# Attention and gated-FFN block on one core: W_k loaded transposed in five blocks, its fold in one stretch, W_q's blocks moved into the loop

## The chip, the core and the metric

The kernel runs on one core of a Trainium2 chip. The metric is device time in microseconds: the median over executions of the whole program. Four executions of the kernel before gave 279.43, 279.59, 280.50 and 281.14 us, with a median of 280.05 us.

A core has five engines that run side by side, each in its own program order: PE (TensorE, matrix products; PEld is its weight load), DVE (VectorE), ACT (ScalarE), POOL (GpSimd) and SP (SyncE). In this kernel all transfers are issued from SP's queue; the profile calls its issuing time SPq. An engine waits for another, or for a transfer, on a semaphore, and everything queued behind a waiting instruction on the same engine waits too.

## The reference

One batch of 2048 rows of width D = 640, in bf16:

```
x = A_x                                    # (1, 2048, 640)
def A(x):                                  # attention, 32 heads of width 20
    q, k, v = split(x @ wqkv)              # each (32 heads, 2048, 20)
    pq, pk = q @ w_phi[h], k @ w_phi[h]    # per head, 20 x 20
    phi_q = concat(softmax(pq), softmax(-pq))
    phi_k = concat(softmax(pk), softmax(-pk))
    kv, z = phi_k^T @ v, sum_s phi_k
    o = (phi_q @ kv) / (phi_q . z + 1e-6)
    return o @ wo
def B(x):
    return (gelu(x @ w_gate) * (x @ w_up)) @ w_down    # F = 1536
h   = x + A(layernorm(x))
out = h + B(layernorm(h))
```

## The kernel before, in words

The 2048 rows are 16 tiles of 128 rows. `x_sb[b]` holds four tiles; `LN1T[b]` holds their layernormed rows transposed, so that the 640 features lie in five chunks of 128 partitions. The first stage, which the change touches, takes up the first 26 us or so; behind it come the rest of a loop over the 16 tiles (k, v and the sum phi_k^T v), the q side, and the attention output woven into the FFN. Those later stages are long runs of matrix products on PE and are not edited, apart from the loop's passes 0 to 4.

**The fold.** The per-head product with `w_phi` is linear, so it is folded into the weights: `Wk2 = W_k · blockdiag(w_phi)`, and `Wq2` likewise. `fold` (L210) takes the weight transposed (`WkT`, `WqT`) and the block diagonals `BD`, which DVE builds from `wphi` and a mask (L391). A fold of one block d of 128 rows is six matmuls into a PSUM tile `wa` and one copy out of it: on ACT for the blocks named in `KA` (`QA` for W_q), otherwise on DVE (L232 to L235). W_k's fold must be over before the first k product; W_q's blocks are folded in passes 4 to 8 (`FQ`).

**Transfers.** SP issues, in this order: tiles 0, 1, 3 of x, W_v in three pieces with tile 2 of x between them, `wphi` (L178), tiles 4 and 5 (L179), the whole of W_k transposed on its way in (L180), tiles 6 and 7 (L181), tiles 8 to 11 (L185), the whole of W_q transposed (L186), tiles 12 to 15 (L187). After that SP issues the transposes of layernormed tiles 6 to 15 (`LN1T`, L148), each of which waits for its tile.

**Tiles 0 to 5.** Their layernormed rows are transposed on PE (`ln_tp`: five transposes into a PSUM tile `tp`, then a copy to `LN1T` on DVE or ACT). `ln_st` is the statistics on DVE with the reciprocal root on ACT (`log=True`) or POOL; `ln_ap` applies them. Tile 3's statistics come from two ACT passes (`st3_act`) and a short POOL chain. v of tiles 0 to 3 is computed ahead of the loop, from PSUM tile `pv` to `vS` on ACT (`v_ev`).

**Order.** All engines run in the order in which the program is written (`manual_schedule`); no planner moves anything. PE's order from tile 2 on is: transposes of tile 2, rest of v(1), part of v(2), transposes of tile 3, rest of v(2), half of v(3), fold of W_k's blocks 0 and 1, other half of v(3), fold of blocks 2 to 4, transposes of tile 4. Pass t of the loop then does k(t), in passes 4 to 8 a fold of W_q, on odd passes from 5 on two tiles of kv, and v(t+4). Pass 0 has tile 5's transposes between k(0) and v(4). Pass t also prepares the layernormed tile t+6: pass 0 on DVE, later ones on ACT. All PSUM tiles of this stage share four buffers in rotation (`gtile`).

Of the kernel before, what the change touches and what calls it, by code (L numbers as in the profile page):

```python
# [10 lines left out]
ALU = mybir.AluOpType  # L11
# [6 lines left out]
def kernel(  # L18
# [12 lines left out]
    nc = tc.nc  # L31
    P = 128
# [13 lines left out]
    NH = [(P * c + P - 1) // Dh - H0[c] + 1 for c in range(NC)]  # L46
    NWARM = 10
    VP = (0, 2, 4, 6, 9, 11)
    KA, QA = (0,3), (0,1,2,3,4)
    FQ = (4, 5, 6, 7, 8)  # L50

    QG = ((0, 1), (2, 3), (4, 5), (6,), (7, 8), (9, 10), (11, 12), (13, 14), (15,), (16,), (17,), (18,), (19,))
# [124 lines left out]
    nc.sync.dma_start(Wv[:, 4:5, :], w_v[:, 4:5, 2 * D:3 * D])  # L177
    nc.sync.dma_start(wphi, phi_v.rearrange("(c p) f -> p c f", p=P))  # L178
    nc.sync.dma_start(x_sb[1][:, 0:2, :], x_v[:, 4:6, :])  # L179
    nc.sync.dma_start_transpose(WkT, A_wqkv[:, D:2 * D])  # L180
    nc.sync.dma_start(x_sb[1][:, 2:4, :], x_v[:, 6:8, :])  # L181
    wo_v = A_wo.rearrange("(c p) n -> p c n", p=P)
    wg_v = B_w_gate.rearrange("(c p) n -> p c n", p=P)
    wu_v = B_w_up.rearrange("(c p) n -> p c n", p=P)
    nc.sync.dma_start(x_sb[2], x_v[:, 8:12, :])  # L185
    nc.sync.dma_start_transpose(WqT, A_wqkv[:, 0:D])  # L186
    nc.sync.dma_start(x_sb[3], x_v[:, 12:16, :])  # L187


    zero = fp.tile([P, 512], BF16, name="zero")  # L190
# [19 lines left out]
    def fold(WT, W2, halves, ds=range(NC)):  # L210


        runs = []
        for c in range(NC):
            lo, hi = H0[c] * Dh, (H0[c] + NH[c]) * Dh
            for u in range(2):
                a, b = max(lo, u * HD), min(hi, (u + 1) * HD)
                if a < b:
                    runs.append((u, c, a, b))
        runs.sort()  # L220
        for d in ds:
            wa = gtile("wa")
            for i, (u, c, a, b) in enumerate(runs):
                nc.tensor.matmul(wa[:, u, a - u * HD:b - u * HD], lhsT=WT[:, c, d * P:(d + 1) * P],  # L224
                                 rhs=BD[:, c].rearrange("p a b -> p (a b)")[:, a - H0[c] * Dh:b - H0[c] * Dh],
                                 start=(i == 0 or runs[i - 1][0] != u),
                                 stop=(i + 1 == len(runs) or runs[i + 1][0] != u), skip_group_check=True)
            dst, src = W2[:, d, :].rearrange("p (u f) -> p u f", u=2), wa[:, :, 0:HD]
            if halves:
                dst = W2[:, d, :].rearrange("p (c u f) -> p u c f", c=NC, u=2)  # L230
                src = src.rearrange("p u (c f) -> p u c f", c=NC)
            if d in (QA if halves else KA):  # L232
                nc.scalar.copy(dst, src)
            else:
                nc.vector.tensor_copy(dst, src)  # L235
# [3 lines left out]
    def ln_st(*tiles, act=True, between=None, log=False):  # L239
        for t, v in zip(tiles, ln_stats(p1, [x_sb[t // 4][:, t % 4, :] for t in tiles], "1", act, between, log)):  # L240
            lnp[t] = v

    def ln_ap(t, on_act=False, on_pe=False):
        ln = (ln_act if on_act else ln_dve)(p1, "1", *lnp[t])
        if on_pe:
            lnp[t] = ln
        else:
            transpose_to(LN1T[t // 4][:, :, t % 4 * P:(t % 4 + 1) * P], ln, False)

    def ln_tp(t, on_dve=False):  # L250
        transpose_to(LN1T[t // 4][:, :, t % 4 * P:(t % 4 + 1) * P], lnp[t], True, on_dve)
# [13 lines left out]
    def v_mm(t, us=(0, 1)):  # L265
        if 0 in us:
            pv[t] = gtile("pv")
        proj(pv[t], t, Wv, us)

    def v_part(t, *cs):  # L270

        if 0 in cs:
            pv[t] = gtile("pv")
        for c in cs:
            for u in range(2):
                nc.tensor.matmul(pv[t][:, u, 0:HD], lhsT=lnT(t, c), rhs=Wv[:, c, u * HD:(u + 1) * HD],
                                 start=(c == 0), stop=(c == NC - 1))

    def v_ev(t):
        nc.scalar.copy(vS[t % 8][:, :, 0:Dh].rearrange("p (u h) f -> p u h f", u=2),  # L280
                       pv[t][:, :, 0:HD].rearrange("p u (h f) -> p u h f", f=Dh))
# [13 lines left out]
    def k_norm(t):  # L295


        sk = small(p1, [P, 2 * H], "sk")
        nc.vector.reduce_sum(sk, Ek[t].rearrange("p s (h f) -> p (s h) f", f=Dh), axis=AX.X)  # L299
        if t - 1 in todo:  # L300
            todo.pop(t - 1)()
        rs = small(p1, [P, 2 * H], "rs")
        nc.vector.reciprocal(rs, sk)  # L303
        Vt[t] = vt = ev.tile([P, 2, H, VC], BF16, name="vt", bufs=8)

        def mult(s, eng):
            eng.tensor_tensor(vt[:, s], vS[t % 8], rs[:, s * H:(s + 1) * H, None].to_broadcast([P, H, VC]), ALU.mult)  # L307

        mult(1, nc.gpsimd)
        if t in VP:  # L310
            mult(0, nc.gpsimd)
        elif t == NT - 1:
            mult(0, nc.vector)
        else:
            todo[t] = lambda: mult(0, nc.vector)
# [38 lines left out]
    def st3_act(i):  # L354

        xt = x_sb[0][:, 3, :]
        nc.scalar.activation(sq3, xt, (ACTF.Square, ACTF.Identity)[i], accum_out=sm3[:, i:i + 1])
        if i == 1:
            nc.gpsimd.tensor_scalar(v3[:, 0:1], sm3[:, 1:2], sm3[:, 1:2], -1.0 / (D * D), op0=ALU.mult, op1=ALU.mult)
            nc.gpsimd.tensor_scalar_add(v3[:, 0:1], v3[:, 0:1], EPS)  # L360
            nc.gpsimd.tensor_scalar(v3[:, 1:2], sm3[:, 0:1], 1.0 / D, v3[:, 0:1], op0=ALU.mult, op1=ALU.add)
            nc.gpsimd.tensor_tensor(v3[:, 2:3], v3[:, 1:2], nhalf[:, 0:1], op=ALU.pow)
            nc.gpsimd.tensor_scalar(v3[:, 3:4], sm3[:, 1:2], 1.0 / D, None, op0=ALU.mult)
            lnp[3] = xt, v3[:, 3:4], v3[:, 2:3], None
# [2 lines left out]
    sm3 = fp.tile([P, 2], F32, name="sm3")  # L367
    v3 = fp.tile([P, 4], F32, name="v3")

    def st1_between():  # L370
        st3_act(0)
        ln_ap(0, on_pe=True)

    ln_st(0, act=False, log=True)
    ln_st(1, act=False, between=st1_between, log=True)
    st3_act(1)
    ln_tp(0, True)
    warm(WA)
    ln_ap(1, on_pe=True)
    v_part(0, 0, 1)  # L380
    ln_tp(1)
    ln_st(2, act=False, log=True)
    v_part(0, 2, 3, 4)
    v_ev(0)
    v_part(1, 0, 1, 2)
    ln_ap(2, on_pe=True)
    ln_ap(3, on_pe=True)
    ln_tp(2, True)
    ln_st(4, act=False)

    nc.vector.tensor_tensor(BD, wphi[:, :, None, :].to_broadcast([P, NC, 8, Dh]),  # L391
                            hmask[:, :, :, None].to_broadcast([P, NC, 8, Dh]), ALU.mult)
    v_part(1, 3, 4)
    v_ev(1)
    v_part(2, 0, 1)
    ln_tp(3)
    v_part(2, 2, 3, 4)
    v_ev(2)
    ln_ap(4, on_pe=True)
    ln_st(5, act=False)  # L400
    v_mm(3, (0,))
    fold(WkT, Wk2, False, (0, 1))
    v_mm(3, (1,))
    v_ev(3)
    fold(WkT, Wk2, False, (2, 3, 4))
    ln_ap(5, on_pe=True)
    ln_tp(4)
    ln_st(6)
    ln_st(7)
    fp_cm.__exit__(None, None, None)  # L410
    ev_cm = tc.tile_pool(name="ev", bufs=1, side="right", reuse_waits="tile")
# [2 lines left out]
    for t in range(NT):  # L414
        if t == T3:
            ps_cm.close()
            psG = ps_cm.enter_context(tc.tile_pool(name="psG", bufs=3, space=PSUM, reuse_waits="tile"))
            psK = ps_cm.enter_context(tc.tile_pool(name="psK", bufs=1, space=PSUM, reuse_waits="tile"))
            kvp = psK.tile([P, 2, 512], F32, name="kvp")
        k_tile(t)  # L420
        if t == 0:
            ln_tp(5)
            ln_ap(6)
        if t in FQ:
            fold(WqT, Wq2, True, [i for i, f in enumerate(FQ) if f == t])
        for j in range(len(QT)):
            if t == QT[j]:
                q_mm(j)
                q_exp(j)
        if t % 2 == 1 and t >= 5:  # L430
            kv_tile(t - 5)
            kv_tile(t - 4)
        if t + 4 < NT:
            v_mm(t + 4)
        if t > 0 and t + 6 < NT:
            ln_ap(t + 6, on_act=True)
        if t + 4 < NT:
            v_ev(t + 4)
        if t % 2 == 0 and t + 8 < NT:
            ln_st(t + 8, t + 9)  # L440
        k_norm(t)
        if t == 9:
            nc.gpsimd.memset(KV, 0.0)
            nc.gpsimd.memset(kmask, 1.0)
            for r in HALF:
                nc.gpsimd.affine_select(out=kmask[r], in_=kmask[r], pattern=[[4, NC], [-Dh, 4]],
                                        compare_op=ALU.is_ge, fill=0.0, base=0, channel_multiplier=1)
                nc.gpsimd.affine_select(out=kmask[r], in_=kmask[r], pattern=[[-4, NC], [Dh, 4]],
                                        compare_op=ALU.is_ge, fill=0.0, base=Dh - 1, channel_multiplier=-1)
            nc.gpsimd.tensor_copy(KV[:, :, 0, :, KC - 1], kmask)  # L450
            nc.gpsimd.tensor_copy(KV[:, :, 1, :, 0], kmask)
        if t == 10:
            nc.sync.dma_start(Wg, wg_v)
            nc.sync.dma_start(Wo, wo_v)
            nc.sync.dma_start(Wu, wu_v)
# [282 lines left out]
```

The softmax here doesn't subtract the row's maximum and nothing guards it: scores larger than these inputs give would overflow.

## Time and profile before

The profiled execution took 281.14 us, the longest of the four; its span, first to last instruction, is 279.40 us, so 1.74 us lie around it.

| what | value |
|---|---|
| median of 4 runs | 280.05 us |
| profiled execution, and its span | 281.14 us, 279.40 us |
| PE busy | 272.1 us, 97% of the span |
| DVE, ACT, POOL busy | 165.1, 143.0, 95.7 us |
| granted TensorE clock | 1.00 |
| DMA queue of SP | 20.68 MB, 30.5% of 16 engines |

How to read it: a row of the timeline gives the start and the length in us, the engine, the source line, what is written from what, and in brackets how long the engine had been idle and who ended that. A row's length of several matmuls includes the drain of the last one, so successive rows can overlap. "To landing" is the time from the start of a transfer's issue on SP until its last piece has been signalled. The chain of work that ended last is followed back from the last instruction: a piece on it that gets shorter shortens the span unless another chain takes over.

### The profile page before, as it was taken

Reading aid. Unit: us, or ns where it says so; the run is one execution under the profiler, and the core shown is the slowest. Engines: PE = TensorE matmul, PEld = TensorE weight load, DVE = VectorE, ACT = ScalarE, POOL = GpSimd, SP = SyncE. Lnnn points to the kernel's source line nnn. Section 1 sums busy time; section 2 is a strip of 40 time slices with the busy share of each in tenths; the row PEclk is TensorE's granted clock in tenths of the full one; section 3 lists DMA queues with packets and bytes.
Section 4 is the critical chain, followed back from the end, with each engine's and each line's share of the span. In section 5 each row is a group of like instructions: output and inputs, shape, how many; then the busy total and the mean of one; then the engine's idle time right before and its main releaser. Section 6 shows DMA issues by size and latency. Waiting matters only on the chain.

```text
span 279.4 us, 5780 instructions
## 1 busy us (share of the span) xinstructions
PE 272.1 (97%) x2322; PEld 172.4 (62%) x2337; DVE 165.1 (59%) x289; ACT 143.0 (51%) x239; POOL 95.7 (34%) x211
## 2 busy tenths in 40 slices
PE   7898999999999999999999999999999999999995
PEld 3575777774645788788864555675455567444574
DVE  5699997789397686676324848322657632333222
ACT  5577999768598847355624454412446350222200
POOL 3438996694401315555401244310135230000000
PEclk9999999999999999999999999999999999999999
DMA  7997122694350021314120113131031513000011
GB/s 210 179 228 179 38 48 49 148 395 189 95 191 0 2 48 26 69 38 99 34 70 2 32 21 69 38 82 47 2 47 23 74 25 94 26 0 0 0 49 47
DMA packets 40635, 21.05 MB, mean 75 GB/s; under 512 B 33440, under 2 KB 38816, under 8 KB 40608
## 3 DMA queue, kind: packets, MB, share of 16 engines
q1 hardware_dynamic: 40608, 20.68, 30.5%
q8 instruction: 18, 0.29, 0.4%
q14 instruction: 9, 0.07, 0.1%
HBM read 10.18 MB, written 2.62 MB: 46 GB/s over the span
## 4 chain that ended last, share of the span: by engine, by line
PE 89%; DMA 4%; DVE 3%; SPq 1%; POOL 1%; issue 1%; POOLq 0%
PE gu L588 37%; PE pd L609 19%; PE pq L347 8%; PE po L543 8%; PE pk L260 6%; PE pv L260 5%; PE ab L483 3%; PE kvp L325 2%; DMA x_sb<-in_A_x_dram 2%; DMA LN1T<-ln 2%; DVE stats L108 1%; DVE Wk L235 1%; PE wa L224 1%; DVE ln L137 0%; POOL rstd L121 0%
## 5 line engine op out<-in xcount | busy, mean ns | idle before, releaser
L594 DVE TENSOR_TENSOR GT<-gu,g 128x512 bf16<-128x512 f32 (+1 forms) x60 | 34.4, 580 | 54.3 <-ACT g L591 54.1
L591 ACT ACTIVATE g<-gu 128x512 bf16<-128x512 f32 (+1 forms) x60 | 30.7, 512 | 69.4 <-PE gu L588 68.2
L588 PE MATMUL gu<-LN2T,Wg 128*128 128x512 bf16 (+1 forms) x289 | 61.3, 335 | 0.7
L588 PE MATMUL gu<-LN2T,Wu 128*128 128x512 bf16 (+1 forms) x300 | 61.7, 336 | 0.0
L609 PE MATMUL pd<-Wd,GT 128*128 128x320 bf16 (+2 forms) x396 | 53.8, 295 | 0.0
L609 PEld LDWEIGHTS <-GT 128*128 128x128 bf16 x396 | 38.0, 98 | 15.3 <-DVE GT L594 0.9
L588 PEld LDWEIGHTS <-Wu 128*128 128x128 bf16 x300 | 29.4, 98 | 22.6
L588 PEld LDWEIGHTS <-Wg 128*128 128x128 bf16 x300 | 28.4, 98 | 20.7
L260 PEld LDWEIGHTS <-LN1T 128*128 128x128 bf16 x290 | 27.6, 98 | 12.4 <-DMA LN1T<-ln 1.5
L307 POOL TENSOR_TENSOR vt<-vS,rs 128x672 bf16<-128x672 bf16 x22 | 29.7, 1372 | 9.2 <-DVE rs L303 8.5
L614 DVE TENSOR_TENSOR y<-pd,x_sb 128x640 bf16<-128x640 f32 (+3 forms) x18 | 13.5, 749 | 30.2 <-PE pd L609 30.2
L491 ACT COPY AB<-ab 128x704 f32<-128x704 f32 x28 | 19.6, 748 | 19.8 <-PE ab L483 19.6
L299 DVE TENSOR_REDUCE sk<-E 128x64 f32<-128x1280 bf16 x16 | 23.1, 1446 | 4.2 <-ACT E L292 4.2
L524 DVE TENSOR_TENSOR tt<-AB,w 128x1280 bf16<-128x1280 f32 x16 | 23.8, 1485 | 1.1 <-POOL w L517 0.9
L543 PE MATMUL po<-Wo,oT 128*128 128x320 bf16 x160 | 24.3, 299 | 0.0
L260 PE MATMUL pk<-Wk,LN1T 128*128 128x320 bf16 x160 | 24.2, 299 | 0.0
L292 ACT ACTIVATE E<-pk 128x640 bf16<-128x640 f32 x32 | 20.9, 707 | 6.5 <-PE pk L260 6.3
L347 PE MATMUL pq<-LN1T,Wq 128*128 128x512 bf16 x96 | 22.7, 379 | 0.2
L260 PE MATMUL pv<-Wv,LN1T 128*128 128x320 bf16 x130 | 20.0, 299 | 1.2 <-DMA LN1T<-ln 1.2
L352 ACT ACTIVATE Eq<-pq 128x1024 bf16<-128x1024 f32 (+1 forms) x26 | 19.9, 830 | 2.4 <-PE pq L347 2.4
L543 PEld LDWEIGHTS <-oT 128*128 128x128 bf16 x160 | 15.6, 98 | 7.0 <-ACT oT L146 0.3
L132 ACT ACTIVATE ln<-x_sb,v,rstd 128x640 bf16<-128x640 bf16 x14 | 12.9, 919 | 11.3 <-POOL v L571 11.1
(89 smaller groups left out, 264.0 us busy)
## 6 DMA issues: line engine op xcount, KB each, us to landing
out_dram<-y SPq DMA_DIRECT2D x15, 160.0 KB, 1.8
Wg<-in_B_w_gate_dram SPq DMA_DIRECT2D x1, 1920.0 KB, 7.6
Wu<-in_B_w_up_dram SPq DMA_DIRECT2D x1, 1920.0 KB, 14.9
Wd<-in_B_w_down_dram SPq DMA_DIRECT2D x1, 1920.0 KB, 7.9
x_sb<-in_A_x_dram SPq DMA_DIRECT2D x2, 640.0 KB, 5.5
Wo<-in_A_wo_dram SPq DMA_DIRECT2D x1, 800.0 KB, 9.3
x_sb<-in_A_x_dram SPq DMA_DIRECT2D x4, 160.0 KB, 2.8
Wv<-in_A_wqkv_dram SPq DMA_DIRECT2D x2, 320.0 KB, 4.1
```

Source lines behind the costliest of these rows:

```text
L260: nc.tensor.matmul(ps[:, u, 0:HD], lhsT=lnT(t, c), rhs=W[:, c, u * HD:(u + 1) * HD], start=(c == 0), stop=(c == NC - 1))
L292: nc.scalar.activation(Ek[t][:, s, :].rearrange("p (u f) -> p u f", u=2), pk[:, :, 0:HD], ACTF.Exp, scale=(1.0 if s == 0 else -1.0))
L299: nc.vector.reduce_sum(sk, Ek[t].rearrange("p s (h f) -> p (s h) f", f=Dh), axis=AX.X)
L307: eng.tensor_tensor(vt[:, s], vS[t % 8], rs[:, s * H:(s + 1) * H, None].to_broadcast([P, H, VC]), ALU.mult)
L347: nc.tensor.matmul(pqs[j][:, i, :], lhsT=Wq2[:, kc, c * P:(c + 1) * P], rhs=LN1T[b][:, kc, :], start=(kc == 0), stop=(kc == NC - 1))
L352: nc.scalar.activation(Eq[j][:, :, s, :], pqs[j][:, 0:len(QG[j])], ACTF.Exp, scale=(1.0, -1.0)[s])
L524: nc.vector.tensor_tensor(tt.rearrange("p s (h f) -> p s h f", f=Dh), num, w[:, :, :, None].to_broadcast([P, 2, H, Dh]), ALU.mult)
L543: nc.tensor.matmul(po[:, u, 0:HD], lhsT=st[t][:, c, :], rhs=Wo[:, c, u * HD:(u + 1) * HD], start=(c == 0), stop=(c == NC - 1))
L588: nc.tensor.matmul(gu[:, i, 0:n], lhsT=W[:, c, f * P:(f + 1) * P], rhs=LN2T[b][:, c, a0:a1], start=(c == 0), stop=(c == NC - 1))
L591: nc.scalar.activation(g[:, 0:n], gu[:, 0, 0:n], ACTF.Gelu_apprx_tanh)
L594: nc.vector.tensor_tensor(st[b, "g", f][:, a0:a1], gu[:, 1, 0:n], g[:, 0:n], ALU.mult)
L609: nc.tensor.matmul(pd[:, u, n0:n1], lhsT=st[b, "g", f][:, tl * P:(tl + 1) * P], rhs=Wd[:, f, u * HD + n0:u * HD + n1], start=(f == 0), sto ...
```

## The change

W_k is loaded transposed by five transfers of 128 rows each in place of one. The loads of tiles 6 to 15 are written behind v(2), but on SP they follow the five W_k blocks directly. W_q is loaded by five such transfers too, one at the end of each of the passes 0 to 4, behind the transpose of layernormed tile t+6 on SP's queue.

The block diagonals are built in two pieces, chunks 0 to 2 and chunks 3 and 4, with tile 2's layernorm between them; both are now ahead of tile 4's statistics on DVE. Tile 3's two ACT passes come later: the first behind tile 1's, the second behind tile 2's reciprocal root. Tile 3's layernorm comes behind tile 4's statistics.

On PE, v(2) is one stretch, then W_k's blocks 0, 1 and 2 are folded, then tile 3's transposes, then blocks 3 and 4, then v(3) in one stretch, then tile 4's transposes; tile 5's transposes come behind v(4) in pass 0. ACT copies out blocks 1 and 3, in place of 0 and 3. On DVE the statistics of tiles 5 and 6 come ahead of the layernorm of tile 5.

```diff
-    KA, QA = (0,3), (0,1,2,3,4)
+    KA, QA = (1,3), (0,1,2,3,4)
...
-    nc.sync.dma_start_transpose(WkT, A_wqkv[:, D:2 * D])
-    nc.sync.dma_start(x_sb[1][:, 2:4, :], x_v[:, 6:8, :])
+
+    def load_T(WT, i, *ds):
+
+        for d in ds:
+            nc.sync.dma_start_transpose(WT[:, :, d * P:(d + 1) * P], A_wqkv[d * P:(d + 1) * P, i * D:(i + 1) * D])
+
+    load_T(WkT, 1, *range(NC))
...
-    nc.sync.dma_start(x_sb[2], x_v[:, 8:12, :])
-    nc.sync.dma_start_transpose(WqT, A_wqkv[:, 0:D])
-    nc.sync.dma_start(x_sb[3], x_v[:, 12:16, :])
...
-    def st1_between():
-        st3_act(0)
-        ln_ap(0, on_pe=True)
+    def bd(c0, c1):
+
+        n = c1 - c0
+        nc.vector.tensor_tensor(BD[:, c0:c1], wphi[:, c0:c1, None, :].to_broadcast([P, n, 8, Dh]),
+                                hmask[:, c0:c1, :, None].to_broadcast([P, n, 8, Dh]), ALU.mult)
 
     ln_st(0, act=False, log=True)
-    ln_st(1, act=False, between=st1_between, log=True)
-    st3_act(1)
+    ln_st(1, act=False, between=lambda: ln_ap(0, on_pe=True), log=True)
+    st3_act(0)
     ln_tp(0, True)
     warm(WA)
     ln_ap(1, on_pe=True)
     v_part(0, 0, 1)
     ln_tp(1)
     ln_st(2, act=False, log=True)
+    st3_act(1)
     v_part(0, 2, 3, 4)
     v_ev(0)
+    bd(0, 3)
+    ln_ap(2, on_pe=True)
+    bd(3, NC)
     v_part(1, 0, 1, 2)
-    ln_ap(2, on_pe=True)
-    ln_ap(3, on_pe=True)
     ln_tp(2, True)
     ln_st(4, act=False)
-
-    nc.vector.tensor_tensor(BD, wphi[:, :, None, :].to_broadcast([P, NC, 8, Dh]),
-                            hmask[:, :, :, None].to_broadcast([P, NC, 8, Dh]), ALU.mult)
+    ln_ap(3, on_pe=True)
     v_part(1, 3, 4)
     v_ev(1)
-    v_part(2, 0, 1)
-    ln_tp(3)
-    v_part(2, 2, 3, 4)
+    v_part(2, *range(NC))
     v_ev(2)
+    nc.sync.dma_start(x_sb[1][:, 2:4, :], x_v[:, 6:8, :])
+    nc.sync.dma_start(x_sb[2], x_v[:, 8:12, :])
+    nc.sync.dma_start(x_sb[3], x_v[:, 12:16, :])
+    fold(WkT, Wk2, False, (0, 1, 2))
+    ln_tp(3, False)
+    fold(WkT, Wk2, False, (3, 4))
+    v_mm(3)
+    v_ev(3)
     ln_ap(4, on_pe=True)
+    ln_tp(4)
     ln_st(5, act=False)
-    v_mm(3, (0,))
-    fold(WkT, Wk2, False, (0, 1))
-    v_mm(3, (1,))
-    v_ev(3)
-    fold(WkT, Wk2, False, (2, 3, 4))
+    ln_st(6)
     ln_ap(5, on_pe=True)
-    ln_tp(4)
-    ln_st(6)
     ln_st(7)
...
         if t == 0:
-            ln_tp(5)
             ln_ap(6)
...
             v_mm(t + 4)
+            if t == 0:
+                ln_tp(5)
...
         k_norm(t)
+        if t < NC:
+            load_T(WqT, 0, t)
```

## The prediction, made before the changed kernel was run

> **What bounds the kernel now.** I read the page first, for who carries the span: PE, busy 97%. So time can only come from the few places where PE stands still. The second view is the chain that ended last, in order of time: from 25.29 us on it is PE alone, without a wait worth naming, and ahead of that it runs through transfers and DVE.
>
> ```profile
> PE 272.1 (97%) x2322; PEld 172.4 (62%) x2337; DVE 165.1 (59%) x289; ACT 143.0 (51%) x239; POOL 95.7 (34%) x211
> ```
>
> ```profile
> 4.63 6.37 DMA x_sb<-in_A_x_dram
> 11.00 0.02 issue
> 11.02 0.90 DVE stats L108 x2
> ...
> 20.31 4.93 DMA LN1T<-ln
> 25.25 0.05 issue
> 25.29 1.53 PE pv L260 x10
> 26.82 1.36 PE pk L260 x10
> ```
>
> So the span is 25.29 us plus a PE stream that the change leaves as long as it is; what counts is when v(6), the product at 25.29, can start. The timeline of PE shows the two stalls before it, 0.80 us for W_k transposed and 1.16 us for tile 6's transpose:
>
> ```profile
> 13.97 0.80 PE L224 MATMUL wa<-BD,WkT 128*128 128x140 bf16 x12 [0.80 <-DMA WkT<-in_A_wqkv_dram]
> ...
> 22.61 1.52 PE L260 MATMUL pk<-Wk,LN1T 128*128 128x320 bf16 x10
> 25.29 1.53 PE L260 MATMUL pv<-Wv,LN1T 128*128 128x320 bf16 x10 [1.16 <-DMA LN1T<-ln]
> ```
>
> SP's queue tells why. The two whole transposes hold SP for 6.74 and 5.66 us, x's last tiles are issued only at 18.78, and tile 6's transpose at 20.31 lands 4.93 us later where the next two took 2.6:
>
> ```profile
> 5.20 6.74 SPq L180 DMA_TRANSPOSE WkT<-in_A_wqkv_dram  x1
> 11.99 0.57 SPq L181 DMA_DIRECT2D x_sb<-in_A_x_dram  x1
> 12.60 0.43 SPq L185 DMA_DIRECT2D x_sb<-in_A_x_dram  x1
> 13.07 5.66 SPq L186 DMA_TRANSPOSE WqT<-in_A_wqkv_dram  x1
> 18.78 0.58 SPq L187 DMA_DIRECT2D x_sb<-in_A_x_dram  x1
> ```
>
> Last, the rows of tile `wphi`, for the new position of the block diagonals. It lands at 4.15 + 5.6 = 9.75 us:
>
> ```profile
> L178 SPq DMA_DIRECT2D wphi<-in_A_w_phi_dram x1: 433/433/433, 4.2 to 4.2; - x1
> ...
> DMA to landing us min/median/max: 5.6/5.6/5.6
> ```
>
> **The change, step by step.** All times are in the profiled execution (281.14 us, span 279.40, 1.74 around it). The pace of PE is from the chain: a v or k product 1.36, a folded block 0.32, five transposes 0.28.
>
> *Block diagonals ahead of tile 2's layernorm.* DVE is done with tile 2's statistics at 8.15. It then waits for `wphi` until 9.77; before, it could go on at 8.99, when ACT's root was ready. Behind the wait are tile 2's layernorm, the second piece, the copy of tile 2's transposes and tile 4's statistics; PE waits for the first. The whole takes 0.94 us for 800 elements. For 480 I bound it by 0.56 (proportional) and 0.94 (no cheaper than the whole), and take 0.60, nearer the proportional end, since the width falls by two fifths. So: piece one 9.77 to 10.37, layernorm (0.45) to 10.79, and PE's transposes of tile 2 start at 10.85 instead of 9.50. By the rows of before the copy starts 0.55 after the layernorm's end and takes 0.49: 11.34 to 11.83. The second piece (0.41) fits while PE transposes. v(2) starts at 11.88 against 10.53: 1.35 us lost here, with PE idle for some 1.25 us from 9.6.
>
> *Tile 4's statistics and tile 3.* Statistics 11.77 to 12.90 (0.89 and 0.21); their data are there at 11.0, so that wait of before is gone. Tile 3's ACT passes end near 9.8, POOL's five steps (7.34 to 9.16 before, 1.82) near 11.7; its layernorm runs at 12.86 to 13.30, where it hides beside v(2). v(0)'s copy moves from 8.87 to 9.8 behind the ACT pass; its buffer is next wanted by v(2), so this costs nothing.
>
> *PE from v(2) on.* v(2) to 13.25; blocks 0 to 2 to 14.21; tile 3's transposes to 14.5; blocks 3 and 4 to 15.14. ACT copies v(2) (0.69), block 1, then tile 3's transposes until 15.34, so v(3) starts at 15.39, a stall of 0.25. It ends at 16.75; transposes of tile 4 (layernorm on DVE at 15.95 to 16.40, behind its third copy of a fold) to 17.03; k(0) from 17.03. Ahead of v(6) PE then has what it had before, k(0), v(4), tile 5's transposes, k(1), v(5) and k(2): 17.03 + 5 × 1.36 + 0.28 = 24.11.
>
> *W_k in five blocks.* SP: each block bounded by 1.20 (a tile's transpose of the same shape) and 6.74/5 = 1.35, so the last is issued by 11.4 to 11.9, against 11.94. The landing of block 4 is bounded below by 10.2 + 2.6 = 12.8 (a lone tile transpose) and, if the bytes come as those of the whole, by 13.9 (5.20 + 8.7). I take 13.9: both share the queue with x. It is wanted at 14.82, block 2 at 13.89, by which the whole would be nearly down. Hidden, with 0.9 us of cover.
> The Trainium skill, "DMA: Bandwidth & Descriptors", section "Anatomy of one DMA", gives each transfer about 2.0 us of fixed cost and so speaks against cutting one transfer into five; charged one after the other, the four more would bring block 4 to an estimated 13.9 + 8.0 = 21.9 us, 7.1 behind its need, and the result to some 6 us slower. This trace has four loads of x and W_v issued within 1.4 us of each other, at 0.79 to 2.18, landing 2.3 to 3.9 us after issue, so such costs overlap here.
>
> *Loads of x.* They follow W_k at 11.4 to 11.9, 12.5 and 13.0. Tiles 12 to 15 are thus issued 5.8 us sooner, and with 5.2 to 5.8 us to landing, as before, are down by 19, ahead of tile 6's transpose.
>
> *Tile 6.* DVE: block 0 copied 13.62 to 14.43, block 2 to 15.15, block 4 to 16.0 (0.81 each, some 0.74 apart), tile 4's layernorm to 16.4, statistics of 5 and 6 to 18.5, layernorm 5, statistics of 7 to 19.85, layernorm 6 to 20.30: the time of before, 20.28, by coincidence. Its transpose is issued at 20.35 with nothing ahead of it; 2.6 us bring it to 22.95, under 24.11 by 1.16. The wait of 1.16 is gone.
>
> *W_q in the loop.* Five issues of 1.20 on SP, each behind the transpose of a tile and ahead of the next one's. ACT ends tile 7's layernorm at 23.57 as before, while SP is free from about 22.8; blocks 1 to 4 likewise fall into the 2 to 4 us between SP's transposes. Block 0 lands near 24.2 and is folded near 29.5, block 4 near 37 and is folded near 43.8. Cost nothing; the cover is SP's gap. Without it a tile transpose comes 1.2 later. Tile 7 lands at 26.2, wanted at 26.83; tile 8 at 28.9, wanted at 29.87. Before, that slack was 1.8 and 2.1 us.
>
> **Sum.** Taken away: stalls of 1.16 and 0.80, and idle ends of early products that the rows show as busy; added: 1.25 at tile 2 and 0.25 at tile 3. All together v(6) goes from 25.29 to 24.11, −1.18 us. ACT, DVE and POOL keep up: DVE works ahead of PE's needs by some 4 us at the kv products, and ACT's passes are as long as before. So 281.14 becomes 279.96. The profiled execution lies 1.09 above the median; the same 1.18 off 280.05 gives 278.9 us, 0.4% less. A difference under 0.5%, 1.4 us, is about what a measurement of this kernel can't tell from none.
>
> **Rivals.**
> *More is won: `wphi` comes sooner.* The stretches from 9.0 to 10.5 us show the transfers nearly idle, 7, 10 and 26 GB/s, with a piece of x and of `wphi` still out, so an execution without that hole is possible. `wphi` can't be sooner than the W_v piece ahead of it, 3.64 + 4.3 = 7.94. At 8.2 v(2) starts at 10.5 as before and the folds are next held by W_k's last block, 13.9: 0.9 us more, 278.0.
> *Given back in the loop.* Slack at tiles 7 and 8 falls to 0.6 and 1.0, and of ten tile transposes before two took 4.2 us to land; one such at tile 7 costs 1.6 − 0.6 = 1.0. Then −0.2: 279.9. Against it: both slow ones came after 30 us.
> *Slower: the five blocks land one after another.* If each block of W_k needed 2.6 us behind the one before, block 4 would land at 5.20 + 5 × 2.6 = 18.2; the fold waits 3.4 us, net +2.2: 282.3. It decides against the change once block 4 lands later than 14.82 + 1.18 = 16.0. For it speaks that no trace row shows two transposes back to back; against it, that the whole moved five blocks in 8.7.
>
> **How the numbers follow.** The forecast, between −0.4 and −1.9 us (278.1 to 279.7): 0.58. More won: 0.15. Given back, 279.7 to 280.5: 0.14. Slower by 1.4 and up: 0.13. The range leaves out the slower case and a few hundredths below: 277.5 to 281.0. Faster by over 0.5% (under 278.65) are two fifths of the forecast and all of the first rival, 0.23 + 0.15 = 0.38; slower 0.13; the rest, 0.49, lies within.
>
> **What would show it.** DVE waiting for the `wphi` transfer for about 1.6 us ahead of the first piece; PE idle near 9.6 to 10.9 for tile 2's layernorm; the waits of PE for W_k and for tile 6 gone; k(0) at about 17.0, v(6) at about 24.1; tile 6's transpose landing in 2.6. Wrong would be: a wait of the folds for a W_k block, a wait of a v product for a tile, or W_q's blocks delaying the tile behind them.

## The result, and the profile after

The changed kernel takes 279.15 us (median of 53 executions, 278.87 to 279.74). The kernel before, measured over 79 executions beside it, takes 279.47 us, not the 280.05 of the four shown; its executions spread from 278.96 to 282.01, and 15 of them lie above 280.4. The ratio is 0.9982, with a 95% interval of 0.9974 to 0.9990; neither here nor below is it simply the quotient of the medians, which is 0.9989 here. The gain is 0.3 us (0.1%) between the medians and 0.5 us (0.2%) between the means, clear of noise but within the half per cent. The fastest executions of the two are 0.1 us apart; what the change removes is above all the late ones: none of these 53 lies above 280.4, and 24 of the 79 lie above the slowest of the 53.

The profiled execution of the changed kernel took 279.19 us with a span of 277.5, against 281.14 and 279.4: 1.9 us, six times the difference of the medians. The busy times of its page, and the timeline of PE with its waits up to k(3):

```profile
PE 271.6 (98%) x2322; PEld 172.4 (62%) x2337; DVE 165.8 (60%) x290; ACT 142.8 (51%) x239; POOL 95.5 (34%) x211
```

```profile
7.95 1.79 PE L278 MATMUL pv<-Wv,LN1T 128*128 128x320 bf16 x12 [0.39 <-DMA Wv<-in_A_wqkv_dram]
9.72 0.45 PE L145 MATMUL tp<-ident,ln 128*128 128x128 bf16 x5
10.02 2.28 PE L278 MATMUL pv<-Wv,LN1T 128*128 128x320 bf16 x14
12.13 1.11 PE L226 MATMUL wa<-BD,WkT 128*128 128x140 bf16 x18
...
16.08 1.52 PE L262 MATMUL pk<-Wk,LN1T 128*128 128x320 bf16 x10
...
23.15 1.52 PE L262 MATMUL pv<-Wv,LN1T 128*128 128x320 bf16 x10
24.51 1.52 PE L262 MATMUL pk<-Wk,LN1T 128*128 128x320 bf16 x10
```

Both stalls of before are gone but for 0.21 us at W_k's last block: v(6) follows k(2) without a wait at 23.15, 2.14 us sooner than the 25.29 of before; k(0) starts at 16.08 against 16.72. From v(6) to the end of the span it takes 254.35 us against 254.11, so 0.24 of the gain is lost again behind it. SP's queue and DVE show the new order (x5 are the five blocks of W_k, issued one after the other):

```profile
5.20 6.93 SPq L184 DMA_TRANSPOSE WkT<-in_A_wqkv_dram  x5
12.18 0.58 SPq L401 DMA_DIRECT2D x_sb<-in_A_x_dram  x1
12.80 0.43 SPq L402 DMA_DIRECT2D x_sb<-in_A_x_dram  x1
13.27 0.43 SPq L403 DMA_DIRECT2D x_sb<-in_A_x_dram  x1
19.61 1.21 SPq L148 DMA_TRANSPOSE LN1T<-ln  x1
20.86 1.28 SPq L184 DMA_TRANSPOSE WqT<-in_A_wqkv_dram  x1
22.77 1.20 SPq L148 DMA_TRANSPOSE LN1T<-ln  x1
```

```profile
8.65 0.66 DVE L375 TENSOR_TENSOR BD<-wphi,hmask 128x480 bf16<-128x480 bf16 x1 [0.57 <-DMA wphi<-in_A_w_phi_dram]
9.23 0.44 DVE L137 TENSOR_SCALAR ln<-x_sb,mv,rstd 128x640 bf16<-128x640 bf16 x1
9.59 0.48 DVE L375 TENSOR_TENSOR BD<-wphi,hmask 128x320 bf16<-128x320 bf16 x1
```

DVE does wait for `wphi`, but 0.57 us and not 1.6: the transfer landed 4.4 us after its issue here, 5.6 in the profile of before. The last load of x is issued at 13.27 in place of 18.78 and lands 7.7 us later, at 21.0 in place of 24.6. Tile 6's transpose, issued at 19.61, takes 2.6 us. Five blocks of W_k hold SP for 6.93 us.

### The profile page after: what moved, and what is told of

Read it like the earlier page. It is cut to its first block, busy times and chain, and to the rows that moved or that the text cites. A ratio compares the mean times of both kernels' runs of the same rounds, so it can differ in the third digit from the quotient of the medians.

```text
span 277.5 us, 5793 instructions
## 1 busy us (share of the span) xinstructions
PE 271.6 (98%) x2322; PEld 172.4 (62%) x2337; DVE 165.8 (60%) x290; ACT 142.8 (51%) x239; POOL 95.5 (34%) x211
## 4 chain that ended last, share of the span: by engine, by line
PE 95%; DMA 2%; ACT 1%; SPq 1%; issue 1%; DVE 0%
PE gu L596 38%; PE pd L617 19%; PE pq L349 8%; PE po L551 8%; PE pk L262 7%; PE pv L262 6%; PE ab L491 3%; PE kvp L327 2%; DMA Wv<-in_A_wqkv_dram 2%; PE pv L278 1%; PE wa L226 1%; PE tp L145 1%; ACT ln L132 0%; ACT E L294 0%; ACT vS L282 0%
```

## The experiments

No kernel below leaves out any of the computation. "Before" beside each is the kernel before, run on the same chip.

### How usual was the profile of before?

The kernel before, unchanged, profiled once more. Two theories stood against each other: the prediction's profile was of a late execution (theory 1), or the gain at v(6) is real in every execution and is given back later (theory 2).

> The kernel before, unchanged, profiled once more. Theory 1: the profiled execution of before that the prediction was built on was one of its late ones (281.14 against a median of 279.47 over 79 runs), because its first transfers came late; a usual execution has wphi down within 5.0 us of its issue, tiles 4 and 5 within 5.5 (6.4 in the shown one) and v(6) at 23.5 to 24.2 us. Theory 2: every execution of before has v(6) near 25.3, and the changed kernel gives its gain back later than v(6).

It took 279.38 us. From the timelines of PE and SP in this second profile:

```profile
12.89 0.79 PE L224 MATMUL wa<-BD,WkT 128*128 128x140 bf16 x12
...
15.24 0.47 PE L224 MATMUL wa<-BD,WkT 128*128 128x140 bf16 x6 [0.25 <-DVE Wk L235]
...
21.86 1.52 PE L260 MATMUL pk<-Wk,LN1T 128*128 128x320 bf16 x10
23.54 1.53 PE L260 MATMUL pv<-Wv,LN1T 128*128 128x320 bf16 x10
```

```profile
5.19 5.11 SPq L180 DMA_TRANSPOSE WkT<-in_A_wqkv_dram  x1
10.35 0.57 SPq L181 DMA_DIRECT2D x_sb<-in_A_x_dram  x1
10.97 0.42 SPq L185 DMA_DIRECT2D x_sb<-in_A_x_dram  x1
11.44 5.46 SPq L186 DMA_TRANSPOSE WqT<-in_A_wqkv_dram  x1
16.95 0.58 SPq L187 DMA_DIRECT2D x_sb<-in_A_x_dram  x1
```

`wphi` landed after 4.2 us, tiles 4 and 5 after 4.5 (6.4 in the first profile), W_k after 7.1 (8.7). W_k held SP for 5.11 us in place of 6.74, the last load of x went out 1.8 us sooner, and the fold started at 12.89 without a wait for W_k. Of the two stalls the prediction counted on, 0.80 and 1.16 us, the first is absent and the second is down to 0.3 (k(2) starts at 21.86 and takes 1.36; v(6) starts at 23.54). From v(6) to the end it takes 277.7 − 23.54 = 254.2 us as in the first profile. Theory 1 holds, theory 2 falls: the changed kernel's v(6) is only 0.39 us ahead of this one. Tile 6's transpose, issued at 19.57, took 3.9 us here against 4.93 in the first profile.

Can a delay of the first transfers make such an execution? One more load, 384 KB of w_gate that is loaded again later, was put ahead of `wphi`:

```diff
+    nc.sync.dma_start(Wg[:, 0:1, :], B_w_gate.rearrange("(c p) n -> p c n", p=P)[:, 0:1, :])
     nc.sync.dma_start(wphi, phi_v.rearrange("(c p) f -> p c f", p=P))
```

> The kernel before with one more load, 384 KB of w_gate, issued ahead of wphi; the later load of w_gate overwrites it, and the result is the same. It makes the first transfers late on purpose: some 0.5 us on SP and some 1.3 us of transfer. Theory 1, the late executions of before are those whose first transfers are late, and the delay goes through tiles 4 and 5, W_k, W_q and tiles 12 to 15 to tile 6's transpose: tiles 4 and 5 down near 10.5 to 11.5 (9.1 in the second profile of before), v(6) at 24.8 to 25.8, 280.6 to 281.6. Rival, a delay of the first transfers is absorbed before tile 6: 279.4 to 279.9, v(6) under 24.2.

280.46 us against 279.32, ratio 1.0042 (1.0026 to 1.0059).

```profile
22.21 1.52 PE L261 MATMUL pk<-Wk,LN1T 128*128 128x320 bf16 x10
24.57 1.53 PE L261 MATMUL pv<-Wv,LN1T 128*128 128x320 bf16 x10 [0.84 <-DMA LN1T<-ln]
```

Tiles 4 and 5 were down at 5.10 + 5.5 = 10.6, the last load of x went out at 18.08, tile 6's transpose landed after 4.6 us and v(6) came at 24.57, a little short of the range expected (24.8 to 25.8, 280.6 to 281.6). The rival, that the delay is absorbed, is out: the 1.1 us arrive at the end. The edit does not copy the first profile exactly, though. Of the 1.13 us by which the last load of x goes out later than in the second profile, 0.57 is the added issue on SP itself (W_k starts at 5.76, not 5.19) and 0.56 the longer hold of W_k (5.67, not 5.11); in the first profile W_k starts on time and its longer hold gives nearly all of it. That the late executions of before had late first transfers is seen in the first profile only; others were not profiled.

### Which part of the change counts?

The kernel before with W_q alone moved:

```diff
-    nc.sync.dma_start_transpose(WqT, A_wqkv[:, 0:D])
...
         k_norm(t)
+        if t < NC:
+            nc.sync.dma_start_transpose(WqT[:, :, t * P:(t + 1) * P], A_wqkv[t * P:(t + 1) * P, 0:D])
```

> The kernel before with one edit: W_q in five blocks of 128 rows, one at the end of each of the passes 0 to 4, in place of the whole. Theory 1, W_q's place is the larger part of the gain: the median falls by 0.2 to 0.5 us to 279.0 to 279.3 and the late executions go, v(6) waits for no transfer. Rival, the gain is W_k's blocks and the order: 279.4 to 279.6, unchanged.

279.15 us (278.85 to 279.46, 11 executions), ratio 0.9982 (0.9970 to 0.9995): the whole gain of the change. Twelve of the 23 executions of before beside it are slower than the slowest of these 11, but only one of the 23 lies above 280.4, so this run alone does not show that the latest ones are gone. v(6) starts at 23.40 directly behind k(2).

```profile
22.04 1.52 PE L259 MATMUL pk<-Wk,LN1T 128*128 128x320 bf16 x10
23.40 1.52 PE L259 MATMUL pv<-Wv,LN1T 128*128 128x320 bf16 x10
...
28.83 0.48 PE L223 MATMUL wa<-BD,WqT 128*128 128x140 bf16 x6
```

The other way round, the changed kernel with W_q whole again at its old place:

```diff
     nc.sync.dma_start(x_sb[2], x_v[:, 8:12, :])
+    nc.sync.dma_start_transpose(WqT, A_wqkv[:, 0:D])
     nc.sync.dma_start(x_sb[3], x_v[:, 12:16, :])
...
-        if t < NC:
-            load_T(WqT, 0, t)
```

> The changed kernel with W_q loaded transposed in one piece between tiles 8 to 11 and 12 to 15 of x, as before, and not in the loop. Theory 1, the gain is W_q leaving the way of tile 6's transpose: PE waits for that transpose again, v(6) moves from 23.15 to 24.0 or later, time 279.6 to 280.4. Rival, W_q's place does not matter in a usual execution and the gain is in the order on PE and DVE: 279.1 to 279.3, no such wait.

282.62 us, ratio 1.0115 (1.0083 to 1.0147): far beyond the 279.6 to 280.4 expected. The direction of theory 1 was right, its size was not. Its SP queue and PE:

```profile
5.20 6.79 SPq L184 DMA_TRANSPOSE WkT<-in_A_wqkv_dram  x5
12.03 0.58 SPq L401 DMA_DIRECT2D x_sb<-in_A_x_dram  x1
12.65 0.42 SPq L402 DMA_DIRECT2D x_sb<-in_A_x_dram  x1
13.12 7.45 SPq L403 DMA_TRANSPOSE WqT<-in_A_wqkv_dram  x1
20.62 0.58 SPq L404 DMA_DIRECT2D x_sb<-in_A_x_dram  x1
```

```profile
26.16 1.53 PE L262 MATMUL pv<-Wv,LN1T 128*128 128x320 bf16 x10 [2.84 <-DMA LN1T<-ln]
```

W_q now starts on SP at 13.12 instead of 11.44 and holds it for 7.45 us; the last load of x goes out 3.7 us later than in the second profile of before, and tile 6's transpose lands 4.8 us after 21.32. So W_k's blocks, which here hold SP for 6.79 us against 5.11 for the whole, should do much of this harm by themselves. The kernel before with W_k's blocks alone:

```diff
-    nc.sync.dma_start_transpose(WkT, A_wqkv[:, D:2 * D])
+    for d in range(NC):
+        nc.sync.dma_start_transpose(WkT[:, :, d * P:(d + 1) * P], A_wqkv[d * P:(d + 1) * P, D:2 * D])
```

> The kernel before with one edit: W_k in five blocks of 128 rows on SP, W_q whole at its old place. Theory 1, the blocks hold SP for 6.8 us against some 5 for the whole, so W_q, tiles 12 to 15 and tile 6's transpose all come 1.7 to 2.2 us later: v(6) at 25.5 to 26.5, 281.5 to 283. Rival, the 3.5 us of the changed kernel with W_q whole came from the new order on the other engines: 279.4 to 280.

281.28 us, ratio 1.0088 (1.0064 to 1.0112), v(6) at 25.28 behind a wait of 1.93 us for tile 6, slightly under the range; SP is held for 6.57 us.

```profile
5.20 6.57 SPq L181 DMA_TRANSPOSE WkT<-in_A_wqkv_dram  x5
...
25.28 1.53 PE L261 MATMUL pv<-Wv,LN1T 128*128 128x320 bf16 x10 [1.93 <-DMA LN1T<-ln]
```

W_k in blocks, alone, costs 1.9 us. The run before it lost 3.1 us, and the other 1.2 stay open; in its profile W_q held SP for 7.45 us, here for 6.82. And the changed kernel with W_k whole:

```diff
-    load_T(WkT, 1, *range(NC))
+    nc.sync.dma_start_transpose(WkT, A_wqkv[:, D:2 * D])
```

> The changed kernel with W_k loaded transposed in one piece. Theory 1, the early fold needs the blocks: the whole lands 7.8 to 8.7 us after its issue, at 13.0 to 13.9, the first fold moves from 12.13 to 13.1 or later, and as PE has no gap behind it the end moves by as much: 279.8 to 280.6. Rival, the last block is what counts and it lands at the same time either way: at most 0.2 us, 279.1 to 279.4.

279.19 us (278.92 to 280.85), ratio 0.9991 (0.9975 to 1.0006).

```profile
5.19 4.71 SPq L186 DMA_TRANSPOSE WkT<-in_A_wqkv_dram  x1
...
11.97 1.12 PE L226 MATMUL wa<-BD,WkT 128*128 128x140 bf16 x18
```

Theory 1 fails: with W_k whole the fold started at 11.97, no later than 12.13, for the whole took 6.7 us to land here (5.19 to 11.9) and held SP for 4.71 us. The rival has the time right but not the reason, since the last of five blocks landed at 14.0. The profiled execution is the fastest of its 12, 278.92, and its W_k the earliest of six, so it may not be the usual one. So blocks in place of the whole win nothing that can be measured in the median. One of 12 executions, 280.85, was later than any of the 53 of the changed kernel.

The order alone, with both weights whole at their old places:

```diff
-    load_T(WkT, 1, *range(NC))
+    nc.sync.dma_start_transpose(WkT, A_wqkv[:, D:2 * D])
...
     nc.sync.dma_start(x_sb[2], x_v[:, 8:12, :])
+    nc.sync.dma_start_transpose(WqT, A_wqkv[:, 0:D])
     nc.sync.dma_start(x_sb[3], x_v[:, 12:16, :])
...
-        if t < NC:
-            load_T(WqT, 0, t)
```

> The changed kernel with both weights loaded transposed in one piece at their old places on SP's queue: only the new order on PE, ACT and DVE and the two pieces of the block diagonals are left of the change. Theory 1, all of the gain is W_q leaving the way: tile 6's transpose lands at 23.2 to 23.7, PE wants it at 22.9 and waits 0.2 to 0.8, median 279.3 to 279.6 with late executions above 280. Rival, the order is a gain of its own: 279.1 to 279.2.

279.44 us, ratio 1.0007 (0.9995 to 1.0019), one late execution of 281.2 in 11. The time is theory 1's and the rival is out, but the wait that theory 1 expected is not in this profile: tile 6's transpose landed at 19.91 + 3.1 = 23.0 and PE came for it at 23.52, having waited 1.1 us for W_v early on. The order on PE, ACT and DVE is worth nothing measurable by itself; in this one profile PE, not the transfer, was the later of the two.

### The block diagonals in front of the layernorm

The first piece of the block diagonals behind tile 2's layernorm, the second behind the copy of its transposes:

```diff
-    bd(0, 3)
     ln_ap(2, on_pe=True)
-    bd(3, NC)
+    bd(0, 3)
     v_part(1, 0, 1, 2)
     ln_tp(2, True)
+    bd(3, NC)
```

> The changed kernel with the first piece of the block diagonals behind tile 2's layernorm and the second behind the copy of tile 2's transposes. Theory 1: DVE no longer stands in front of PE, v(2) starts at 10.2 to 10.4 in place of 10.76, but W_k's last block still lands at 14.0, so k(0) gains at most 0.2 (16.08 to 15.9): 279.0 to 279.2. Rival, the piece in front was the bound: 278.7 to 278.9.

279.10 us, ratio 0.9989 (0.9979 to 0.9999): as the changed kernel, theory 1. Here DVE does not wait for `wphi`; the fold starts at 11.79 instead of 12.13, but its last block is still held by the transfer:

```profile
11.79 1.11 PE L226 MATMUL wa<-BD,WkT 128*128 128x140 bf16 x18
...
13.81 0.49 PE L226 MATMUL wa<-BD,WkT 128*128 128x140 bf16 x6 [0.15 <-DMA WkT<-in_A_wqkv_dram]
```

k(0) comes at 15.86 against 16.08. That shows no gain of the edit: a second profile of the changed kernel (the run `after_again` below), in which DVE does wait for `wphi`, 0.41 us, has k(0) at 15.90 and v(6) at 22.97, against 22.93 with the edit. With W_k whole on top of that edit:

```diff
-    load_T(WkT, 1, *range(NC))
+    nc.sync.dma_start_transpose(WkT, A_wqkv[:, D:2 * D])
```

> As the run before it on this list, and W_k in one piece, W_q's blocks in the loop. Theory 1: W_k is down at 11.9 to 12.3 and the block diagonals no longer hold PE, so k(0) starts at 15.5 to 15.8 and v(6) at 22.6 to 22.9: 278.7 to 279.0. Rival, PE is held by tile 3's and tile 4's layernorm instead and nothing is won over 279.15.

279.43 us (278.94 to 280.72), ratio 1.0004 (0.9990 to 1.0019): neither theory as it stood. In its profile W_k took 7.6 us and the fold waited 1.03 us for it.

```profile
12.86 1.12 PE L226 MATMUL wa<-BD,WkT 128*128 128x140 bf16 x18 [1.03 <-DMA WkT<-in_A_wqkv_dram]
```

The new order begins its fold some 1 us sooner than the old, when the whole is at times down (11.9) and at times not (12.8); the first two blocks of the changed kernel land at 5.20 + 4.9 = 10.1 and 6.6 + 4.3 = 10.9. That the late executions of the kernels with the new order and W_k whole (280.85, 281.2, 280.64 and 280.72 in the three runs) come from this wait fits, but was not shown.

### The 0.2 us behind v(6)

In the changed kernel PE stands for some 0.2 us ahead of W_q's first fold, at 28.81, and the chain of work is drawn through ACT there:

```profile
26.67 0.70 ACT E L294
27.37 0.81 ACT ln L132
28.17 0.59 ACT vS L282
28.77 0.04 issue
28.81 0.48 PE wa L226 x6
```

ACT's copy of v(4) was put ahead of that of tile 5's transposes, so that ACT begins sooner:

```diff
             v_mm(t + 4)
-            if t == 0:
-                ln_tp(5)
...
             v_ev(t + 4)
+            if t == 0:
+                ln_tp(5)
```

> The changed kernel as it is, beside the next two on one chip: 279.0 to 279.3, v(6) at 22.8 to 23.4, PE standing for 0.2 us ahead of W_q's first fold near 28.8.

> The changed kernel with the copy of v(4) ahead of the copy of tile 5's transposes on ACT in pass 0; PE's order is the same. Theory 1, the new order made ACT the bound from pass 0 to pass 4 (no idle from 19.28 to 34.8, 2.72 us a pass as on PE, and the chain of the changed kernel runs through ACT just ahead of W_q's first fold): ACT starts 0.3 earlier, the 0.2 us in front of that fold goes, 278.9 to 279.0 against 279.15. Rival, that gap is one of PE's instruction supply: it stays at 0.2 and the time is unchanged.

> The same edit on top of the block diagonals behind tile 2's layernorm (279.10 without it). Theory 1: v(6) at 22.9 and no gap in front of the fold, span 277.0 to 277.1, 278.8 to 278.9. Rival: 279.1.

The changed kernel gave 279.12 us, with the edit 279.19, with the edit on the kernel of the block diagonals behind 279.34. On this chip late executions of before are frequent, 7 of 29 above 280.4 with a median of 279.57, and the changed kernel's ratio is 0.9965 (0.9942 to 0.9987); 11 of its 12 executions took 278.98 to 279.83, and one took 572.12, which is not explained and not in the ratio. With the edit nothing is won, and the fold starts at 28.62, 28.56 and 28.86 behind the same pause. ACT did copy v(4) 0.9 us sooner (18.75 against 19.68), then it waited 0.35 for k(1) (its first exponential at 20.39), and from there its work and PE's are timed as without the edit:

```profile
27.82 0.69 ACT L282 CAST vS<-pv 128x640 bf16<-128x640 f32 x1
28.54 1.30 ACT L294 ACTIVATE E<-pk 128x640 bf16<-128x640 f32 x2
```

In each of the kernels with the new order the pause is 0.22 to 0.23 us, and the fold starts 0.05 to 0.06 us after ACT's copy of v(7) is over (28.51 and 28.56 in this one). In the kernel before with W_q in the loop there is no pause: there the fold starts at 28.83 and that copy ends at 29.0. So that copy need not be over for the fold as such, and whether the fold waits for it in the new order is not shown. In the changed kernel the fold's first weight load is done before the pause, and the idle time behind it is put down to "issue", which is time in which the engine waited for nothing that the profile shows:

```profile
28.45 0.10 PEld L226 LDWEIGHTS <-WqT 128*128 128x128 bf16 x1
...
28.81 0.29 PEld L226 LDWEIGHTS <-WqT 128*128 128x128 bf16 x5 [0.26 <-issue]
```

The rival of the expectation, that the gap is one of PE's instruction supply and stays at 0.2 with the time unchanged, fits what came out. But the edit did not move ACT's copy of v(7) against PE, so it cannot tell the two apart, and the cause of the pause stays open. No kernel tried beats the changed one by more than its interval.

## Why the prediction was right, and where not

The forecast was 278.9 us and within half a per cent; the median is 279.15, inside the forecast's own interval. The sign, the place and the mechanism hold: tile 6's transpose no longer stands behind W_q and x, v(6) waits for no transfer, W_q's blocks cost nothing in the loop. That the time comes out so close is luck, two errors that largely cancel: the base stood 0.58 too high, and the gain was taken 0.86 too large (1.18 against 0.32). Both come from late executions: two of the four timed ones, the profiled one among them, lay above 280.4.

- **The base.** "The same 1.18 off 280.05" took the gain of one late execution and subtracted it from a median. The median of before is 279.47, and in its second profile v(6) stood at 23.54, not 25.29. A usual execution has some 0.3 to 0.4 us to give (0.32 between the medians, 0.39 at v(6)), not 1.18 or more. This is the step that failed.
- **The sum.** The terms it names, 1.16 and 0.80 taken away and 1.25 and 0.25 added, make 0.46; the other 0.72 of the 1.18 are the idle ends of early products, which it does not itemize. From k(0) to v(6) it is exact, 7.08 us against 7.07 measured. All that it missed of v(6) in the profiled execution lies ahead of k(0), which came at 16.08 and not at 17.03.
- **Block diagonals ahead of the layernorm.** Mis-sized for the same reason: DVE waited 0.57 us where 1.62 was reckoned, since `wphi` landed after 4.4 us. The pieces took 0.66 and 0.48, against 0.60 and 0.41. v(2) started at 10.76, not 11.88. In the profiled execution the rival "more is won" was thus what happened: v(6) at 23.15, 2.14 us below 25.29, where the rival had put it at some 2.1.
- **W_k in five blocks.** A block held SP for 1.28 us at the median, between the two bounds (1.20 and 1.35), but the longest for 1.61, and the five for 6.93 where at most 6.74 was taken. The last landed at 14.0, as taken (13.9), but PE came for it at 13.8 and not 14.82, so it was no longer covered: a wait of 0.21.
  The Trainium skill's fixed cost of some 2.0 us for each transfer ("DMA: Bandwidth & Descriptors", "Anatomy of one DMA") is given there for transfers issued from GpSimd, while these are issued from SP. Here no such cost adds up one after the other: the five landed 4.9 to 3.1 us after issues some 1.4 apart, the last at 14.0 and not at the 21.9 of that estimate.
  What the cut did cost was SP's time, 6.6 to 7.0 us against 4.7 to 5.6 for the whole, the first profile of before left out; the kernel before with the blocks alone pays 1.9 us for it. The prediction had that queue cost at nothing, because it compared with the 6.74 of a late execution; it did no harm only because W_q leaves the queue in the same change.
- **Loads of x.** The last one was to be down by 19, ahead of tile 6's transpose. It landed at 21.0, after 7.7 us and not 5.2 to 5.8, behind the issue of that transpose at 19.61. It did no harm: the transpose landed at 22.2 all the same.
- **A PE stream that stays as long as it is.** Short by 0.2 us, the pause ahead of W_q's first fold. That ACT keeps up is neither confirmed nor refuted by it.
- **Rivals.** Nothing was given back at tiles 7 and 8, whose transposes took 2.6 us; their slack was 0.5 and 1.0 us, against 0.6 and 1.0. The blocks did not land one after another.

## What to carry to other kernels

A stall in one profile is worth what it costs in the usual execution: look first where the profiled execution stands among the timed ones, and if it is a late one, discount the transfers that came late in it. A large transfer that is needed late should not stand in the issuing queue ahead of small ones that are needed soon; moving W_q alone gave all of this change's gain in the median. Not tried was the smaller edit, W_q whole but behind the last load of x; it could give the same. Cutting a transfer lets its reader begin sooner but can hold the issuing queue longer, and everything behind it pays.

## What was not expected of the hardware

W_k whole, the same instruction issued at the same time, held SP for 4.71, 4.78, 5.11, 5.38, 5.57 and 6.74 us in six profiles, and landed after 6.7, 6.8, 7.1, 7.4, 7.6 and 8.7: the time for which a transposing transfer holds SP rises with the time to its landing, it is not a fixed price. Each of the six landed some 2.0 us after SP was free again. W_q whole shows the same trend, from 5.46 us held and 9.1 to landing up to 7.45 and 10.4, but with 2.9 to 3.7 us between. In five blocks W_k's bytes held SP for 6.57 to 6.99 in seven profiles.

Tile 6's transpose landed 0.5 to 0.8 us after the last load of x in all six profiles with W_q whole, however long that was after its own issue (3.1 to 4.9 us); the first profile of before, for one, has 24.6 and 25.2. In the kernels with W_q's blocks in the loop that load is down by 21.0 or sooner, and the transpose takes its 2.6. All 14 profiles fit one reading: the transpose does not land sooner than some 0.5 us behind the last load of x, and W_q whole keeps that load from being issued. No run moves that load alone.
